# Top-k attention into a gated feed-forward: two score units in one visit of the matrix engine, and a new split of the PSUM banks

## The chip, the cores and the metric

The kernel runs on one core of one Trainium2 chip. A core has a matrix engine (TensorE, "PE" in the profile, with its weight loads as "PEld"), a vector engine (VectorE, "DVE"), a scalar engine (ScalarE, "ACT"), a general engine (GpSimd, "POOL") and DMA queues. Matrix products land in PSUM, a small memory of eight banks of 512 float32 columns on each of 128 partitions. The metric is the device time of one execution in microseconds (us), as the median of several runs; lower is better.

## The reference, cut to what matters

```python
# attention: batch 8, heads 8, sequence S = 576, head_dim D = 64, top_k = 32
scores = np.matmul(q, k.transpose(0, 1, 3, 2)) / np.sqrt(D)
kth    = np.partition(scores, -top_k, axis=-1)[..., -top_k:-top_k + 1]
scores = np.where(scores >= kth, scores, -1e9)
attn   = np.exp(scores - scores.max(-1, keepdims=True))
attn   = attn / (attn.sum(-1, keepdims=True) + 1e-9)
x      = np.matmul(attn, v)             # then (B, H, S, D) -> (4608 tokens, 512)
# feed-forward: w_in (512, 2048), w_out (2048, 512)
h   = x @ w_in
g   = h * np.cos(h)
out = g @ w_out
```

All of it is float32. The kernel works in *units*: 128 tokens times one pair of heads, 36 tiles of tokens times 4 pairs, 144 units in all. Each unit needs 128 x 576 scores for each of its two heads, the 32nd largest score of every row, a softmax over what is kept, and a product with `v`. Four units give a block of 128 tokens by 512 columns for the feed-forward, which is cut into *items*: 8 items of the first kind per block (`x @ w_in`, 8 matmuls of 128 columns each) and 8 of the second kind (`g @ w_out`, 2 matmuls of 512 columns each).

## The kernel before: the parts that the change touches

The program is a chain of *slots*, one for each unit. In slot i the vector engine searches the top 32 of unit i, the scalar engine masks and exponentiates unit i-1, the general engine normalises unit i-2 and splits it into 16-bit halves, the DMA transposes unit i-3, and in every odd slot the matrix engine multiplies two older units with `v`. The scores of unit i+1 are made and taken in the same slot. Items of the feed-forward fill the rest of the matrix engine. Each engine runs its instructions in the order in which this code lists them.

```python
def scores(u):                                   # one PSUM tile of four banks, one buffer
    sc = u["sc"] = ps.tile([P, 2, 2, 512], F32, tag="sc", bufs=1)
    for h in range(2):                           # halves of 288 keys
        for j in range(2):                       # the two heads, rows 0-63 and 64-127
            ...
            nc.tensor.matmul(sc[r0:r0 + rows, j, h, 0:HS], st["q"][d, q0:q0 + rows],
                             st["k"][d, h * HS:(h + 1) * HS], start=True, stop=True)

def take_scores(u):                              # one copy of 2 x 576 to SBUF
    nc.scalar.copy(out=s..., in_=u["sc"]...[:, :, 0:HS])

def values(us):                                  # P@V of two units into one bank of the "mm" pool
    o = us[0]["o"] = ps.tile([P, 512], F32, tag="mm", bufs=4)
    ...
def take_values(us):                             # xT <- that bank, 256 columns
    nc.scalar.copy(out=blk["xT"]..., in_=us[0].pop("o")[:, 0:n * P])

def ff1(blk, i):                                 # first kind; two items fill one bank
    if part % 2 == 0:
        blk["mm"] = ps.tile([P, 512], F32, tag="mm", bufs=4)
    ...                                          # 8 matmuls of 128 columns
    if part % 2: full.append((take_first, ...))  # the bank waits to be taken
def ff2(blk, i, f0):                             # second kind; eight items fill one bank
    if f0 == 0:
        blk["o"] = ps.tile([P, 512], F32, tag="mm", bufs=4)
    ...                                          # 2 matmuls of 512 columns
def take_banks():                                # scalar-engine copies of all full banks:
    while full: ...                              # g <- mm (first kind) or ob <- o (second)

def feed(n):                                     # up to n items, kinds in turn
    ff["tick"] += 1
    while n > 0 and ff["credit"] >= 1:
        ...
        ff["kind"] = 1 - kind
        n, ff["credit"] = n - 1, ff["credit"] - 1

def slot(i, u, w, x, y, z):                      # z: two older units, in odd slots
    if x: reciprocal(x)                          # DVE: first work of the slot, needs den(x)
    topk_first(u, w); ...; topk_round(u, 3)      # DVE: folds (read sc and s), searches
    if z: values(z)                              # PE
    else: feed(1)                                # PE
    scores(units[i + 1])                         # PE
    bounds(w); mask(w)                           # ACT: nb, nd, then two masks
    take_banks()                                 # ACT
    if z: take_values(z)                         # ACT
    take_scores(units[i + 1])                    # ACT
    exponentials(w)                              # ACT: two exps, then den
    ...
    transposes(y); gate(1); normalise(x); split(x); write_halves(x)
    feed(2); take_banks()                        # PE, then ACT
    reduce_first(); reduce_second()              # POOL: range reduction for the cosine
    feed(3)                                      # PE
    sines(2)                                     # ACT: x <- sin of a reduced tile, or of two

for i in range(NU + 1):
    ff["credit"] = min(ff["credit"] + 4.1, 5.0)
    ...
```

Of the kernel before, what the change touches and what calls it, by code (L numbers as in the profile page):

```python
# [10 lines left out]
F32 = mybir.dt.float32  # L11
# [6 lines left out]
P = 128  # L18
# [13 lines left out]
def kernel(  # L32
# [9 lines left out]
    nc = tc.nc  # L42
    ctx.enter_context(tc.manual_schedule())
    B, H, D, S = qT.shape
# [48 lines left out]
        w_out.append(w)  # L93
        chunks.append((moe_w_out[f * P : (f + 1) * P, :], w))
    CHUNKS, XB = 8, 4
    ff = {"live": 0, "tick": 0, "now": 0, "credit": 0.0, "end": False, "kind": 0}

    wq = {"next": 0, "loaded": deque(), "second": deque(), "third": deque(), "done": 0, "ready": 0}

# [92 lines left out]
    def load_v(b, hp):  # L192
# [7 lines left out]
        for j in range(2):  # L200
# [2 lines left out]
                in_=v[b, MAIN:S, hp * P + j * D : hp * P + (j + 1) * D],  # L203
            )

    def scores(u):
        sc = u["sc"] = ps.tile([P, 2, 2, 512], F32, tag="sc", name="sc", bufs=1)
        for h in range(2):
            for j in range(2):
                d = slice(j * D, (j + 1) * D)  # L210
                for b, q0, rows, r0 in u["parts"]:
                    st = pairs[b, u["hp"]]
                    nc.tensor.matmul(  # L213
                        sc[r0 : r0 + rows, j, h, 0:HS],
                        st["q"][d, q0 : q0 + rows],
                        st["k"][d, h * HS : (h + 1) * HS],
                        start=True,
                        stop=True,
                    )

    def take_scores(u):
        s = u["s"] = work.tile([P, 2, S], F32, tag="s", name="s", bufs=4)
        nc.scalar.copy(  # L223
            out=s.rearrange("p j (h w) -> p (j h) w", h=2),
            in_=u["sc"].rearrange("p j h w -> p (j h) w")[:, :, 0:HS],
        )
        if not u["folds"]:
            del u["sc"]

    def fold(u, op):  # L230


        s, sc = u["s"], u["sc"]
        if op == ALU.max:
            u["rest"] = work.tile([P, 2, S], F32, tag="rest", name="rest", bufs=1)
        else:
            del u["sc"]
        i = int(op == ALU.min)
        nc.vector.tensor_tensor(  # L239
            out=u["rest"][:, :, i * HS : (i + 1) * HS], in0=sc[:, :, 0, 0:HS], in1=s[:, :, HS:S],  # L240
            op=op,
        )

# [126 lines left out]
    def transposes_now(u):  # L370

        s = u.pop("s").rearrange("p j k -> p (j k)")
        tp = ps.tile([P, 2, 2, 512], F32, tag="sc", name="tp", bufs=1)
        tt = ps.tile([P, 512], F32, tag="mm", name="tt", bufs=4)
        for c in range(2 * NT + 1):
            j, k = divmod(c, NT + 1)
            to = tt[:, 0:P] if c == NT else tp[:, 0, j, k * P : (k + 1) * P]
            nc.tensor.transpose(to, s[:, c * P : (c + 1) * P], ident)
        pT = u["pT"] = work.tile([P, 2 * NT + 1, P], F32, tag="pT", name="pT", bufs=3)
        for j in range(2):  # L380
            at = j * (NT + 1)
            nc.scalar.copy(
                out=pT[:, at : at + NT].rearrange("p c q -> p (c q)"), in_=tp[:, 0, j]
            )
        nc.scalar.copy(out=pT[:, NT], in_=tt[:, 0:P])

    def values(us):


        o = us[0]["o"] = ps.tile([P, 512], F32, tag="mm", name="o", bufs=4)  # L390
        for i, u in enumerate(us):
            pT = u.pop("pT")
            for b, _, rows, r0 in u["parts"]:
                st = pairs[b, u["hp"]]
                r = slice(r0, r0 + rows)
                to = slice(i * P + r0, i * P + r0 + rows)
                for c in range(NT + 1):
                    for j in range(2):
                        d = slice(j * D, (j + 1) * D)
                        if c < NT:  # L400
                            lhsT, rhs = st["v"][:, c, d], pT[:, j * (NT + 1) + c, r]
                        else:
                            lhsT, rhs = st["v_tail"][:, d], pT[:, NT, r]
                        nc.tensor.matmul(o[d, to], lhsT, rhs, start=c == 0, stop=c == NT)  # L404

    def take_values(us):
        blk, hp, n = block_of[us[0]["tok"]], us[0]["hp"], len(us)
        if "xT" not in blk:
            blk["xT"] = work.tile([P, NP, P], F32, tag="xT", name="xT", bufs=5)
        nc.scalar.copy(  # L410
            out=blk["xT"][:, hp : hp + n].rearrange("p h q -> p (h q)"),
            in_=us[0].pop("o")[:, 0 : n * P],
        )
        blk["left"] -= n
        blk["tick"] = ff["tick"]
# [21 lines left out]
    sined = deque()  # L437
    full = deque()

    def ff1(blk, i):  # L440
        w = blk["w"]
        nf = 256 // w
        part = i % 4
        if part == 0:
            blk["g"].append(ffw.tile([P, 1024], F32, tag="g", name="g", bufs=CHUNKS))
            ff["live"] += 1
        if part % 2 == 0:
            blk["mm"] = ps.tile([P, 512], F32, tag="mm", name="mm", bufs=4)
        g, mm = blk["g"][-1], blk["mm"]
        for a in range(nf):  # L450
            f = i * nf + a
            at = (part % 2 * nf + a) * w
            for c in range(NC):
                nc.tensor.matmul(  # L454
                    mm[:, at : at + w],
                    w_in[f // FC][:, c, (f % FC) * P : (f % FC + 1) * P],
                    blk["xT"][:, c],
                    start=c == 0,
                    stop=c == NC - 1,
                )  # L460
        if part % 2 == 0:
            return
        full.append((take_first, blk, g, mm, part // 2))

    def take_first(blk, g, mm, half):
# [55 lines left out]
    def ff2(blk, i, f0):  # L521
        w = blk["w"]
        if f0 == 0:
            blk["o"] = ps.tile([P, 512], F32, tag="mm", name="o2", bufs=4)
        o = blk["o"]
        per = 1024 // w
        for f in range(f0, f0 + 2):
            g = blk["g"][f // per]
            at = (f % per) * w + i * P
            nc.tensor.matmul(  # L530
                o, g[:, at : at + P], w_out[f], start=f == 0, stop=f == NF - 1
            )
        if f0 + 2 < NF:
            return
        full.append((take_second, blk, i, o))

    def take_second(blk, i, o):
# [23 lines left out]
    def feed(n):  # L561

        ff["tick"] += 1
        while n > 0 and ff["credit"] >= 1:
            for kind in (ff["kind"], 1 - ff["kind"]):
                if (can_first, can_second)[kind]():
                    break
            else:
                return
            if kind == 0:  # L570
                ff1(*first.popleft())
            else:
                ff2(*second.popleft())
            ff["kind"] = 1 - kind
            n, ff["credit"] = n - 1, ff["credit"] - 1

    last = {}  # L580
    for i, u in enumerate(units):
        for part in u["parts"]:
            last[part[0], u["hp"]] = i
    at_slot = {}
    order = [(b, hp) for b in range(B) for hp in range(NP)]
    for n in range(NP, len(order)):
        i = last[order[n - 5]] - 1 if n >= 5 else 0
        at_slot.setdefault(max(i, NP + 2), []).append((load_qk, *order[n]))
        i = last[order[n - 6]] if n >= 6 else 0
        at_slot.setdefault(max(i + 5 - i % 2, NP + 2), []).append((load_v, *order[n]))  # L590

    for hp in range(NP):
# [1 line left out]
    for hp in range(2, NP):  # L594
        at_slot[hp - 2].append((load_qk, 0, hp))

    EARLY, LAST = 2 * NP, NU - NP

    for i, u in enumerate(units):
        u["n"] = i
# [41 lines left out]
    def slot(i, u, w, x, y, z):  # L644
        if x:
            reciprocal(x)
        if u:
            topk_first(u, w)
            decode_second(2)
        if u:  # L650
            topk_round(u, 1)
            topk_round(u, 2)
            topk_round(u, 3)
        if z:
            values(z)
        else:
            feed(1)
        if i + 1 < NU:
            scores(units[i + 1])

        if w:
            bounds(w)
            mask(w)
        take_banks()
        if z:
            take_values(z)
        if i + 1 < NU:
            take_scores(units[i + 1])
        if w:
            exponentials(w)  # L670
        for load, b, hp in at_slot.get(i, []):
            load(b, hp)
        load_weights(2)
        if y:
            transposes(y)
        gate(1)
        if x:
            normalise(x)
            split(x)
            write_halves(x)  # L680
        feed(2)
        take_banks()
        decode_third()
        decode_first(2)
        reduce_first()
        reduce_second()
        feed(3)
        sines(2)
# [39 lines left out]
        take_values([w])  # L728
        feed(2)

    tt = ps.tile([P, 512], F32, tag="mm", name="warm", bufs=4)
    for _ in range(12):
        nc.tensor.transpose(tt[:, 0:P], ident, ident)
    load_qk(0, 0)
# [4 lines left out]
    decode_first(3)  # L739
    for i in range(NU + 1):  # L740
        ff["end"] = i >= NU
        ff["credit"] = min(ff["credit"] + 4.1, 5.0)
        ff["now"] += 1
        wq["ready"] = wq["done"]
        u, w = (units[i - n] if 0 <= i - n < NU else None for n in range(2))
# [55 lines left out]
```

## Time and profile before

| quantity | value |
|---|---|
| time, median of 3 runs | 1526.04 us (1524.19 to 1526.63) |
| span of the profiled execution | 1522.8 us |
| PE busy | 1433.9 us (94%) |
| DVE busy | 1417.3 us (93%) |
| POOL busy | 1107.0 us (73%) |
| ACT busy | 1069.3 us (70%) |
| mean granted TensorE clock | 0.965 of full speed |

How to read it: "busy" is the time in which an engine has an instruction in execution. Matmuls are pipelined and their ends are modelled, so a busy PE isn't a PE at its peak; for PE the distances between starts say more. The profile counts two PE records for each float32 matmul of the program. A wait in a list of waits is put down to the instruction that came last. In the code above, `[P, 2, 576]` scores are `s`, the row sums `den`, the bounds for the mask `nb`, the feed-forward's copies of a bank `g` (first kind) and `ob` (second kind).

### The profile page before, as it was taken

What the parts mean: (1) busy time and instruction counts of PE and PEld (TensorE: products, weight loads), DVE (VectorE), ACT (ScalarE), POOL (GpSimd) and SP (SyncE); (2) the same over time, 40 slices, a digit from 0 to 9 for tenths busy, and PEclk for the clock granted to TensorE, in tenths of its full rate; (3) what the DMA queues carried; (4) which work ended last, traced back from release to release, by engine and by line L of the source; (5) the groups of instructions that cost most, each with busy time, mean ns of one, the idle gap of its engine ahead of it and who ended that gap; (6) DMA issues with size and microseconds to landing.
All of it is one profiled execution on the core that took longest, in us unless ns stands there. A gap on an engine that the chain in (4) does not pass through costs nothing.

```text
span 1522.8 us, 30130 instructions
## 1 busy us (share of the span) xinstructions
PE 1433.9 (94%) x10360; PEld 1023.1 (67%) x10360; DVE 1417.3 (93%) x4689; ACT 1069.3 (70%) x2120; POOL 1107.0 (73%) x838
## 2 busy tenths in 40 slices
PE   4577798999999999999999999999999999999998
PEld 3464466676767676767676767676767676767575
DVE  7999999999999999999999999999999999999721
ACT  7888667676767677767676777676777777776731
POOL 4777958777878787878787878777777777787600
PEclk6688899999999999999999999999999999999999
DMA  8432365536664655554665455645554456544200
GB/s 271 141 93 83 96 169 166 163 117 160 170 165 111 152 144 165 161 148 137 165 171 138 126 148 165 177 121 159 164 163 132 133 142 167 139 141 114 70 10 14
DMA packets 371754, 212.20 MB, mean 139 GB/s; under 512 B 321296, under 2 KB 337937, under 8 KB 371601
## 3 DMA queue, kind: packets, MB, share of 16 engines
q1 hardware_dynamic: 366192, 200.63, 48.0%
q10 hardware_dynamic: 5408, 9.65, 1.8%
q8 instruction: 81, 1.33, 0.4%
q14 instruction: 73, 0.59, 0.1%
HBM read 45.09 MB, written 87.29 MB: 87 GB/s over the span
## 4 chain that ended last, share of the span: by engine, by line
PE 70%; ACT 13%; DVE 10%; DMA 3%; issue 2%; SPq 1%; POOL 0%; ACTq 0%; POOLq 0%; DVEq 0%
PE mm L454 30%; PE o L530 23%; PE sc L213 8%; PE o L404 8%; DVE top L299 4%; DVE rest L302 3%; ACT s L329 2%; ACT x L511 2%; ACT s L321 2%; DMA pT<-rows 2%; ACT s L223 1%; ACT L511 1%; DVE rest L239 1%; DVE w_out L138 1%; ACT nd L312 1%
## 5 line engine op out<-in xcount | busy, mean ns | idle before, releaser
L299 DVE MAX8 top<-rest 128x8 f32<-128x288 f32 (+1 forms) x1656 | 682.2, 461 | 0.0
L454 PEld LDWEIGHTS mm<-xT,w_in 128*128 128x128 f32 x4608 | 545.0, 193 | 102.2 <-issue 91.8
L454 PE MATMUL mm<-xT,w_in 128*128 128x128 f32 x4608 | 565.2, 278 | 4.3 <-ACT xT L410 4.2
L530 PE MATMUL o<-w_out,g 128*128 128x512 f32 x1152 | 541.8, 603 | 4.0 <-POOL w_out L148 3.9
L302 DVE MATCH_REPLACE8 rest<-top,rest 128x288 f32<-128x288 f32 (+1 forms) x1104 | 495.5, 457 | 0.0
L530 PEld LDWEIGHTS o<-w_out,g 128*128 128x128 f32 x1152 | 203.8, 192 | 201.2 <-issue 193.0
L343 POOL TENSOR_SCALAR s<-s,rden 128x576 f32<-128x576 f32 x288 | 212.9, 751 | 139.3 <-DVE rden L338 139.3
L355 POOL COPY halves<-s 128x2304 uint16<-128x2304 uint16 x132 | 277.8, 2105 | 35.6 <-DMA rows<-halves 28.5
L329 ACT ACTIVATE s<-s,nd 128x576 f32<-128x576 f32 x288 | 220.7, 769 | 0.4
L223 ACT COPY s<-sc 128x1152 f32<-128x1152 f32 x144 | 160.7, 1116 | 84.9 <-PE sc L213 84.7
L321 ACT ACTIVATE s<-s,nb 128x576 f32<-128x576 f32 x288 | 205.4, 760 | 0.0
L213 PE MATMUL sc<-k,q 64*128 64x288 f32 (+1 forms) x1280 | 187.3, 443 | 19.0 <-ACT s L223 8.7
L239 DVE TENSOR_TENSOR rest<-sc,s 128x576 f32<-128x576 f32 x264 | 198.7, 753 | 4.9 <-DVE rden L338 0.4
L518 POOL TENSOR_TENSOR g<-g,x 128x1024 f32<-128x1024 f32 x68 | 161.4, 2375 | 51.6 <-ACT x L511 46.9
L309 ACT ACTIVATE nb<-top 128x4 f32<-128x4 f32 x144 | 29.1, 202 | 233.5 <-DVE top L292 233.2
L404 PE MATMUL o<-pT,v 128*64 128x128 f32 (+1 forms) x2560 | 166.0, 272 | 19.2 <-DMA pT<-rows 10.7
L404 PEld LDWEIGHTS o<-pT,v 128*64 128x64 f32 x2560 | 136.4, 141 | 65.1 <-issue 36.8
L501 POOL TENSOR_TENSOR x<-g,x 128x1024 f32<-128x1024 f32 x68 | 161.0, 2367 | 5.7
L213 PEld LDWEIGHTS sc<-k,q 64*128 64x128 f32 (+1 forms) x1280 | 102.2, 183 | 81.5 <-issue 22.5
L492 POOL TENSOR_SCALAR x<-g 128x1024 f32<-128x1024 f32 x68 | 71.3, 1049 | 89.7 <-ACT g L466 89.7
L466 ACT ACTIVATE g<-mm 128x512 f32<-128x512 f32 x144 | 82.1, 582 | 48.6 <-PE mm L454 48.6
L302 DVE MATCH_VALUE_LOAD rest<-top,rest 128x8 f32 x1104 | 86.4, 78 | 0.0
(52 smaller groups left out, 1014.8 us busy)
## 6 DMA issues: line engine op xcount, KB each, us to landing
rows<-halves SPq DMA_DIRECT2D x132, 576.0 KB, 3.2
out_dram<-ob ACTq DMA_DIRECT2D x36, 256.0 KB, 2.8
q<-in_q_dram SPq DMA_DIRECT2D x31, 288.0 KB, 3.0
st<-in_moe_w_in_dram SPq DMA_DIRECT2D x16, 512.0 KB, 5.2
v<-in_v_dram SPq DMA_DIRECT2D x32, 256.0 KB, 3.1
st<-in_moe_w_out_dram SPq DMA_DIRECT2D x16, 512.0 KB, 3.5
k<-in_k_dram SPq DMA_DIRECT2D x31, 144.0 KB, 3.4
k<-in_k_dram SPq DMA_DIRECT2D x32, 128.0 KB, 3.8
```

The lines of the kernel that those rows point to most:

```text
L213: nc.tensor.matmul(sc[r0 : r0 + rows, j, h, 0:HS], st["q"][d, q0 : q0 + rows], st["k"][d, h * HS : (h + 1) * HS], start=True, stop=True,)
L223: nc.scalar.copy(out=s.rearrange("p j (h w) -> p (j h) w", h=2), in_=u["sc"].rearrange("p j h w -> p (j h) w")[:, :, 0:HS],)
L239: nc.vector.tensor_tensor(out=u["rest"][:, :, i * HS : (i + 1) * HS], in0=sc[:, :, 0, 0:HS], in1=s[:, :, HS:S], op=op,)
L299: nc.vector.max(to[:, j], src[:, j])
L302: nc.vector.match_replace(rest[:, j], to[:, j], src[:, j], NEG)
L321: nc.scalar.activation(out=s[:, j], in_=s[:, j], func=AF.Prelu, bias=nb[:, j, 1:2], scale=SCALE, alpha=FAR)
L329: nc.scalar.activation(out=s[:, j], in_=s[:, j], func=AF.Exp, bias=nd[:, j : j + 1], scale=1.0, accum_out=den[:, j : j + 1],)
L343: nc.gpsimd.tensor_scalar(out=s[:, j], in0=s[:, j], scalar1=rden[:, j : j + 1], scalar2=1.0, op0=ALU.mult, op1=ALU.mult,)
L355: nc.gpsimd.tensor_copy(out=halves, in_=s.rearrange("p (k h) -> p h k", h=2))
L404: nc.tensor.matmul(o[d, to], lhsT, rhs, start=c == 0, stop=c == NT)
L454: nc.tensor.matmul(mm[:, at : at + w], w_in[f // FC][:, c, (f % FC) * P : (f % FC + 1) * P], blk["xT"][:, c], start=c == 0, stop=c == NC - 1,)
L530: nc.tensor.matmul(o, g[:, at : at + P], w_out[f], start=f == 0, stop=f == NF - 1)
```

## The change

Scores get two tiles of two banks, so that two units can be in PSUM at once: 448 of the 576 columns lie in such a tile, and the last 128 lie in a pair of banks called `rim`, which both units share and in which P@V and the late transposes also have their place. Scores are then made for two units in one visit of the matrix engine, right behind P@V of two units, in odd slots; in even slots none are made (units of a tile that straddles two sequences are still made one at a time). The purpose is that the matrix engine changes less often between the shapes of attention and those of the feed-forward. The feed-forward is left with two banks, and its items go in twos of a kind, so that a bank of the first kind is filled in one go.

```diff
+    SB = 448
+    rim = ps.tile([P, 2, 512], F32, tag="rim", name="rim", bufs=1)
+    sc_ends = [rim[:, :, i * (S - SB) : (i + 1) * (S - SB)] for i in range(2)]
+    room = [rim[:, j, 2 * (S - SB) :] for j in range(2)]
     def scores(u):
-        sc = u["sc"] = ps.tile([P, 2, 2, 512], F32, tag="sc", name="sc", bufs=1)
-        for h in range(2):
+        sc = u["sc"] = ps.tile([P, 2, 512], F32, tag="sc", name="sc", bufs=2)
+        for to, k0, k1 in ((sc, 0, SB), (sc_ends[u["n"] % 2], SB, S)):
             for j in range(2):
 ...
     def take_scores(u):
-        nc.scalar.copy(out=s.rearrange(...), in_=u["sc"].rearrange(...)[:, :, 0:HS])
+        nc.scalar.copy(out=s[:, :, 0:SB], in_=u["sc"][:, :, 0:SB])
+        nc.scalar.copy(out=s[:, :, SB:S], in_=sc_ends[u["n"] % 2])
 ...
     def values(us):
-        o = us[0]["o"] = ps.tile([P, 512], F32, tag="mm", name="o", bufs=4)
+        o = room[0]
 ...
+    def open_bank():
+        if ff["open"] + len(full) == 2:
+            take_banks()
+        ff["open"] += 1
     def ff1(blk, i):
         if part % 2 == 0:
-            blk["mm"] = ps.tile([P, 512], F32, tag="mm", name="mm", bufs=4)
+            open_bank()
+            blk["mm"] = ps.tile([P, 512], F32, tag="mm", name="mm", bufs=2)
 ...  (ff2 in the same way)
     def feed(n):
-            ff["kind"] = 1 - kind
+            if kind != ff["kind"] or ff["half"]:
+                ff["kind"], ff["half"] = 1 - kind, 0
+            else:
+                ff["half"] = 1
 ...
+        two = i % 2 and EARLY + 2 < i < LAST + 2 and len(u["parts"]) == 1
+        scored.setdefault(i - 2 if two else i - 1, []).append(u)
 ...
     def slot(i, u, w, x, y, z):
         if z:
             values(z)
-        else:
+        made = scored.get(i, [])
+        if not made or not z:
             feed(1)
-        if i + 1 < NU:
-            scores(units[i + 1])
+        for m in made:
+            scores(m)
 ...
-        ff["credit"] = min(ff["credit"] + 4.1, 5.0)
+        ff["credit"] = min(ff["credit"] + 5.0 - 0.9 * len(scored.get(i, [])), 5.3)
```

## The prediction

> **What bounds the kernel now.** I read the busy times over stretches first, then the waits of each engine, then the timeline of one period.
>
> ```profile
> 300.00:500.00 200.00, 199.00 (x1420) 143.44 (x1418) 196.81 (x687) 141.87 (x285) 157.51 (x116) 1.00 0.53 145
> 700.00:900.00 200.00, 198.64 (x1429) 142.33 (x1426) 196.19 (x687) 147.76 (x289) 161.39 (x117) 1.00 0.55 149
> 1440.00:1480.00 40.00, 39.93 (x269) 28.39 (x268) 8.12 (x14) 17.72 (x37) 2.94 (x4) 1.00 0.04 14
> ```
>
> The columns are the stretch, its length, then PE, PEld, DVE, ACT and POOL busy. Between 300 and 1300 us PE shows no gap and DVE is busy for 98.2%: two engines are full at once. After 1440 us the attention is over and PE alone works off the feed-forward's rest.
>
> ```profile
> DVE rden L338 <- ACT den L334: 14.3, 16, 1.3
> DVE rden L338 <- POOL x L493: 0.5, 1, 0.5
> ```
>
> These are all waits of DVE in 1000 us (total, times, longest): only the first instruction of a slot waits, for `den`, and that in 16 slots of about 104. The starts of that reciprocal say the same: 9.50 us apart in nearly every slot, 10.4 to 10.9 once in eight. So a slot costs at least 9.50 us (9.41 after a stall), and 1526 us can shrink only by those stalls: slots 28 to 140 last from 321.1 to 1401.2 us, 1080.1 us for 112 slots, against 112 x 9.50 = 1064. That is 16 us, 1%, however much PE is relieved. The stall, in the timeline:
>
> ```profile
> 811.79 1.28 ACT L511 ACT_TABLE_LOAD   x1
> 813.09 2.19 ACT L511 ACTIVATE x<-x,halfpi 128x1024 f32<-128x1024 f32 x2
> 815.18 0.19 ACT L309 ACTIVATE nb<-top 128x4 f32<-128x4 f32 x1
> 815.79 1.42 ACT L321 ACTIVATE s<-s,nb 128x576 f32<-128x576 f32 x2
> 817.12 0.57 ACT L539 ACTIVATE ob<-o 128x512 f32<-128x512 f32 x1
> 817.73 0.34 ACTq L541 DMA_DIRECT2D out_dram<-ob  x1
> 818.11 0.37 ACT L410 COPY xT<-o 128x256 f32<-128x256 f32 x1 [0.41 <-ACT ob L539]
> 818.38 1.12 ACT L223 COPY s<-sc 128x1152 f32<-128x1152 f32 x1
> 819.52 1.28 ACT L329 ACT_TABLE_LOAD   x1
> 820.81 0.78 ACT L329 ACTIVATE s<-s,nd 128x576 f32<-128x576 f32 x1
> 822.47 0.29 ACT L334 ACTIVATE den<-den,eps 128x2 f32<-128x2 f32 x1
> 822.87 0.17 DVE L338 RECIPROCAL rden<-den 128x2 f32<-128x2 f32 x1 [1.07 <-ACT den L334]
> ```
>
> ACT is 71% busy, but its order is the chain of the slot: `nb`, masks, banks, `xT`, `s`, exps, `den`. After a pair of sines the exps need another table, and with `ob` in the same slot `den` is 1.07 us late.
>
> **What the skill says.** "PSUM — Partial Sum Buffer", section "Engine vs sequencer instructions": the queues of ScalarE, VectorE and GpSimd are strict FIFO. The trace agrees: at 818.11 `xT` starts behind `ob` and the issue of its DMA, though its matmuls were long done (the last began at 816.11). "ScalarE: Activation LUTs", section "What ACT_TABLE_LOAD costs": a load takes about 1283 ns; here 1.28 us. "TensorEngine Tiling (Array Packing)", section "Key Properties": a change of tiling mode drains the engine; that is what the change saves, with the price taken from the trace below. "PSUM — Partial Sum Buffer", section "PSUM bank collisions raise a hardware error": accesses are to be guarded by bank and not by address. The program of before reads and writes different banks, so its trace shows nothing of that; the changed program's waits do.
>
> **The change part by part.**
>
> *PE, removed.* Between items a visit for one unit's scores costs:
>
> ```profile
> 802.22 5.32 PE L530 MATMUL o<-w_out,g 128*128 128x512 f32 x12
> 807.46 1.24 PE L213 MATMUL sc<-k,q 64*128 64x288 f32 x8
> 808.63 1.12 PE L530 MATMUL o<-w_out,g 128*128 128x512 f32 x2
> ```
>
> Starts of single records: 429 ns between two of 512 columns in a run, 522 ns from the last one to the first score; 340 ns for the first pair of scores against 242 for the next; 332 for the last; 533 for the first of the second kind after. The excess is 93 + 98 + 90 + 104 = 385 ns a visit. Counting visits in the program's order: 142 become 84. So 58 x 0.385 = 22 us of PE go, 0.39 us in two slots. The columns are the same: pairs of 448 at 448/288 x 242 = 376 ns and of 128 at 109 (as P@V's pairs), two records each, 970 ns a unit; 4 x 242 = 968 before. Two slots of PE now: P@V 2.33, first unit 1.07 (with its 98), second 0.97, way in and out 0.28, eight items 4 x 1.79 + 4 x 1.72 = 14.03: together 18.68 us, under DVE's 19.0.
>
> *ACT, added.* Two copies for one: 896 columns and 256 at 0.83 ns each plus a start, overlapped as before: 1.06 us for 1.00. The sines come one at a time, at the end of every even slot, not in pairs every fourth: table loads in the program's order go from 74 to 132, 58 x 1.28 = 74 us. ACT has the room, but now every odd slot has a load between `s` and the exps.
>
> *Wait A: `xT` behind both units' scores.* In the changed program the copy to `xT` reads `rim`, and its wait is for the last matmul into `rim`, which is the second unit's end piece. `s` comes behind `xT` in ACT's order. With V the start of P@V: last record at V + 2.33 + 1.07 + 0.86 = V + 4.26, its latency 0.27 and the signal 0.06: `xT` at V + 4.59. Then 0.27 to `s`, 0.79 to the second copy, 0.37 to its end, 1.29 table load, 1.96 exps and `den`, 0.10 to the reciprocal (distances in the trace above): the next slot starts at V + 9.37 or later. Before, `xT` could start at V + 2.46. If P@V starts within 0.1 us of the slot, nothing is lost; every later us is a us of stall.
>
> *Wait B: the first kind has one bank.* Of the two banks, one holds `o2` through eight items. In each fourth slot (the one with `ob`) the order is P@V, scores, then only in the last feed F1 F1 F2, after the last taking of banks. So this F1 bank is copied in the next slot, behind `nb` and the masks; with T that slot's reciprocal, `nb` is at T + 1.85 (832.27 to 834.15 less 0.03), the copy 1.96 later, its end 0.58 later, T + 4.39. The next F1 pair must wait for it: T + 4.45. Behind it PE does F1 F1 (0.10 + 3.57), F2 F2 (3.43), the way into P@V (0.09): V = T + 11.64. The next slot starts at T + 9.5, so P@V is 2.14 us late there, and by wait A the slot after it starts at T + 11.64 + 9.37 = T + 21.01: a stall of 2.0 us.
>
> *Four slots together.* Then 9.45 for the even slot (P@V comes 18.68 after the last, near the start of its slot again), then the `ob` slot: `xT` at 1.85 + 1.96 + 0.57 + 0.42 = 4.80, `s` 5.07, then 0.79 + 0.37 + 1.29 + 1.96 + 0.10: 9.58. Sum 21.01 + 9.45 + 9.58 = 40.04 us for four slots, against 1080.1/28 = 38.58 before: +1.46.
>
> *Sum.* 28 such periods in slots 28 to 140; in three the tile straddles two sequences, scores are made singly, wait A is 0.97 us shorter, so 39.1. 25 x 40.04 + 3 x 39.1 = 1118, less 1080: +38 us. Slots 20 to 27 have the same waits in part: +2. The work left for the end is the same: 33 and 32 items stand behind the last attention matmul. 1526 + 40 = 1566 us.
>
> **Rivals.**
> *PE relieved, DVE reaches its floor.* If wait B were covered, P@V would run ahead, `den` would be in time, and every slot would be 9.5: 1526 - 16 = 1510. For it: PE has 0.3 us to spare in two slots, and the credits and twos look chosen for eight items in two slots. Against it: wait B stands in the order of ACT, and no spare 0.3 us makes up for 2.1.
> *The stalls cancel.* The old stall (1.0 us in eight slots) goes, the new one is smaller because P@V is not as late as I make it or because `xT` needs only P@V: then `s` could start at V + 3.4, 1.4 us earlier, the stall in four slots is 0.6, and the time 1526 within 5 us.
> *More waits.* The sine at the end of an even slot ends at about T + 1.87 of the next, where `nb` wants to start at 1.85; POOL's gate follows it; the transposed halves land some 1.5 us before P@V wants them. If one of these slips, another 0.5 us in four slots: 1580.
>
> **Range and chances.** The working gives 1566. Errors are one-sided in size: full relief is 1510, slips give 1580. I set 1544 to 1580. The line for slower by 2% is 1556.6, that is +31 against my +40; a quarter of my weight is on smaller stalls. Faster by 2% (1495) lies below DVE's floor.
>
> **What would show it.** Reciprocals about 9.5, 11.5, 9.4, 9.6 us apart in turn; `rden` waiting for `den` some 2 us in 28 slots; PE idle before `mm`, with ACT `g` named, 1.7 to 2.4 us in each fourth slot; `xT` starting only behind the second unit's scores; ACT_TABLE_LOAD doubled; score visits at 84. I'm wrong if `xT` starts before the second unit's scores are through, if PE doesn't wait for `g` behind the masks, or if the slots stay at 9.5.

## The result and the profile after

| | before | after |
|---|---|---|
| time, median (of runs of the same comparison) | 1525.12 us | 1596.68 us |
| ratio, 95% interval | | 1.0473 (1.0450 to 1.0496) |
| slots 28 to 140, by the starts of the reciprocal | 1080.1 us | 1148.4 us |
| start of slot 28 / from slot 140 to the end | 321.1 / 121.6 us | 327.5 / 120.2 us |
| ACT_TABLE_LOAD | 74 x 1.28 us | 132 x 1.28 us |

The change makes the kernel 4.7% slower. The prediction had said slower, 1566 us, with 1580 as the upper end; the measured time lies above its range.

The busy times over stretches of the kernel after (stretch, length, then PE, PEld, DVE, ACT, POOL busy, granted TensorE clock, DMA share, GB/s), to be held against the same stretches of before:

```profile
300.00:500.00 200.00, 189.80 (x1309) 136.45 (x1306) 185.20 (x647) 144.25 (x295) 144.58 (x107) 0.97 0.51 143
700.00:900.00 200.00, 189.42 (x1354) 137.62 (x1354) 186.10 (x652) 150.95 (x301) 146.96 (x108) 0.98 0.52 140
```

Neither of the two engines that were full is full any more: PE is at 95%, DVE at 93%, and the clock is no longer 1.00. The waits of the kernel after, over its whole span (engine, line waited for, total us, times, longest), name a ring:

```profile
DVE rden L343 <- ACT den L339: 110.0, 43, 9.1
ACT xT L414 <- PE rim L220: 105.5, 58, 4.5
PE mm L465 <- ACT g L478: 56.6, 32, 1.9
```

DVE waits for ACT (`den`), ACT for PE (`xT` behind the scores' end pieces in `rim`), PE for ACT (the copy `g` that frees the bank of the first kind). Between 300 and 1300 us, the stretch of the list of before in the prediction, the first of these is 73.7 us in 29 waits, against 14.3 in 16. Each engine has long idle times, and each is ended by another engine: such a ring is read by asking which wait is the first in a period. The reciprocals show where the slots get long:

```profile
788.75 0.15 DVE L343 RECIPROCAL rden<-den 128x2 f32<-128x2 f32 x1
800.34 0.17 DVE L343 RECIPROCAL rden<-den 128x2 f32<-128x2 f32 x1 [2.00 <-ACT den L339]
809.75 0.15 DVE L343 RECIPROCAL rden<-den 128x2 f32<-128x2 f32 x1
819.38 0.17 DVE L343 RECIPROCAL rden<-den 128x2 f32<-128x2 f32 x1
828.79 0.15 DVE L343 RECIPROCAL rden<-den 128x2 f32<-128x2 f32 x1
842.00 0.17 DVE L343 RECIPROCAL rden<-den 128x2 f32<-128x2 f32 x1 [3.63 <-ACT den L339]
```

These lines of the timeline (start, length, engine, what) give the slots 11.59, 9.41, 9.63, 9.41, 13.21 us. The pattern is the predicted one (11.5, 9.4, 9.6, then 9.5), but of the late slots 15 take 13.2 to 13.4 us. The PE timeline of such a case, and ahead of it the same wait four slots earlier:

```profile
783.72 3.84 PE L465 MATMUL mm<-xT,w_in 128*128 128x128 f32 x32 [1.93 <-ACT g L478]
787.39 3.60 PE L543 MATMUL o<-w_out,g 128*128 128x512 f32 x8
```

```profile
818.22 3.60 PE L543 MATMUL o<-w_out,g 128*128 128x512 f32 x8
823.75 5.47 PE L465 MATMUL mm<-xT,w_in 128*128 128x128 f32 x32 [1.93 <-ACT g L478]
829.05 3.60 PE L543 MATMUL o<-w_out,g 128*128 128x512 f32 x8
832.58 1.09 PE L408 MATMUL rim<-pT,v 128*64 128x128 f32 x16
836.74 0.39 PE L220 MATMUL rim<-k,q 64*128 64x128 f32 x4
```

and ACT in the stretch of the second one:

```profile
823.12 0.57 ACT L478 ACTIVATE g<-mm 128x512 f32<-128x512 f32 x1
837.18 0.37 ACT L414 COPY xT<-rim 128x256 f32<-128x256 f32 x1 [2.93 <-PE rim L220]
838.65 1.28 ACT L334 ACT_TABLE_LOAD   x1
841.60 0.29 ACT L339 ACTIVATE den<-den,eps 128x2 f32<-128x2 f32 x1
```

`g` ends at 823.69 and PE starts at 823.75 after 1.93 us of idle. The 32 records that follow then take 829.05 - 823.75 = 5.30 us. P@V begins at 832.58, the second unit's end piece comes at 836.74, `xT` at 837.18, and `den` ends 4.7 us after that. In the period before, after the same wait of 1.93 us (783.72), the 32 records took 787.39 - 783.72 = 3.67 us. What differs is in the view of stretches, with the granted clock behind the five busy times:

```profile
783.70:787.10 3.40, 3.38 (x30) 3.39 (x31) 3.40 (x13) 2.84 (x7) 0.75 (x1) 1.00 1.11 299
824.40:827.70 3.30, 3.30 (x18) 3.30 (x17) 3.30 (x13) 2.17 (x7) 0.30 (x1) 0.50 1.15 245
```

The clock was halved for 3.41 us after the second wait, and not after the first. Between slots 28 and 140 there are 16 such windows, in 28 periods; 15 of them lie before a slot of 13.2 to 13.4, the first before one of 11.8 us.

### The profile page after: what moved, and what is told of

Read it like the earlier page. It is cut to its first block, busy times and chain, and to the rows that moved or that the text cites. A ratio compares the mean times of both kernels' runs of the same rounds, so it can differ in the third digit from the quotient of the medians.

```text
span 1596.1 us, 30173 instructions
## 1 busy us (share of the span) xinstructions
PE 1446.7 (91%) x10360; PEld 1041.4 (65%) x10360; DVE 1418.5 (89%) x4689; ACT 1154.5 (72%) x2322; POOL 1104.6 (69%) x838
## 4 chain that ended last, share of the span: by engine, by line
PE 39%; ACT 23%; DVE 20%; POOL 11%; issue 4%; DMA 2%; SPq 1%; DVEq 0%; ACTq 0%; POOLq 0%
PE mm L465 15%; PE o L543 12%; PE rim L408 6%; DVE top L304 6%; DVE rest L244 6%; ACT s L334 5%; DVE rest L307 5%; ACT s L326 5%; PE sc L220 4%; POOL g L530 3%; POOL halves L360 3%; ACT s L230 2%; ACT L334 2%; POOL s L348 2%; ACT nd L317 2%
## 5 line engine op out<-in xcount | busy, mean ns | idle before, releaser
L465 PE MATMUL mm<-xT,w_in 128*128 128x128 f32 x4608 | 586.7, 287 | 64.6 <-ACT g L478 56.6
L465 PEld LDWEIGHTS mm<-xT,w_in 128*128 128x128 f32 x4608 | 561.1, 201 | 122.2 <-ACT g L478 80.5
L543 PE MATMUL o<-w_out,g 128*128 128x512 f32 x1152 | 522.4, 596 | 6.1 <-POOL w_out L148 4.0
L543 PEld LDWEIGHTS o<-w_out,g 128*128 128x128 f32 x1152 | 208.8, 191 | 218.1 <-issue 208.0
L408 PEld LDWEIGHTS rim<-pT,v 128*64 128x64 f32 x2560 | 136.4, 142 | 78.8 <-ACT nb L314 22.7
L408 PE MATMUL rim<-pT,v 128*64 128x128 f32 (+1 forms) x2560 | 164.7, 274 | 23.5 <-ACT pT L389 13.4
L220 PE MATMUL sc<-k,q 64*128 64x448 f32 (+1 forms) x640 | 149.8, 591 | 14.5 <-DMA k<-in_k_dram 8.7
L230 ACT COPY s<-sc 128x896 f32<-128x896 f32 x144 | 129.3, 898 | 6.8 <-PE sc L220 6.8
L343 DVE RECIPROCAL rden<-den 128x2 f32<-128x2 f32 x144 | 22.5, 156 | 111.2 <-ACT den L339 110.0
L414 ACT COPY xT<-rim 128x256 f32<-128x256 f32 (+1 forms) x78 | 27.6, 354 | 119.6 <-PE rim L220 105.5
```

Source lines behind the costliest of these rows:

```text
L220: nc.tensor.matmul(to[r0 : r0 + rows, j, 0 : k1 - k0], st["q"][d, q0 : q0 + rows], st["k"][d, k0:k1], start=True, stop=True,)
L465: nc.tensor.matmul(mm[:, at : at + w], w_in[f // FC][:, c, (f % FC) * P : (f % FC + 1) * P], blk["xT"][:, c], start=c == 0, stop=c == NC - 1,)
L543: nc.tensor.matmul(o, g[:, at : at + P], w_out[f], start=f == 0, stop=f == NF - 1)
```

## The experiments

The theory after the result: two waits make a late slot of 11.6 us (A: `xT` behind both units' scores; B: the first kind's bank copied behind the next slot's masks), and B's idle time costs PE half its clock in 16 of 28 cases. The rivals: the doubled table loads or wait A set the slot whatever the bank does; the extra 1.6 us of the longest slots come from elsewhere. All ratios are to the kernel before.

| run | what it changes in the kernel after | us | ratio (95% interval) | slots 28 to 140, us |
|---|---|---|---|---|
| e1_take_at_end | all banks taken also at a slot's end | 1525.68 | 1.0002 (0.9995 to 1.0009) | 1077.1 |
| e2_keep_busy | PE kept busy through wait B | 1576.33 | 1.0337 (1.0322 to 1.0353) | 1124.6 |
| e3_xT_behind_one | `xT` behind one unit's scores | 1544.77 | 1.0132 (1.0117 to 1.0147) | 1096.1 |
| e4_single_visits | scores of one unit a visit | 1551.99 | 1.0177 (1.0162 to 1.0193) | 1099.7 |
| e5_kinds_in_turn | items one of a kind | 1641.95 | 1.0763 (1.0744 to 1.0781) | 1189.2 |
| e6_first_at_end | first kind taken at a slot's end, and e3 | 1514.68 | 0.9930 (0.9916 to 0.9944) | 1067.7 |
| e7_xT_first | e6, and `xT` ahead of the banks | 1513.75 | 0.9931 (0.9914 to 0.9947) | 1067.2 |
| e8_pairs | e7, and sines in pairs | 1523.16 | 0.9991 (0.9982 to 1.0000) | 1071.6 |
| e9_single_and_end | e10, and scores of one unit a visit | 1526.72 | 1.0006 (0.9997 to 1.0014) | 1076.2 |
| e10_end_alone | first kind taken at a slot's end | 1517.64 | 0.9942 (0.9928 to 0.9956) | 1070.5 |

### The half clock: e2_keep_busy

```diff
         if not made or not z:
             feed(1)
+        if not made and any(f[0] is take_first for f in full):
+            for _ in range(9):
+                nc.tensor.matmul(room[1][:, 0:P], ident, ident, start=True, stop=True)
```

The nine matmuls add work whose results nobody reads; nothing of the kernel is left out.

> The changed kernel with nine matmuls of the identity (results unused, about 2.0 us) on PE in the place where it waits for the bank; the wait itself stays. My theory (14 of the late slots last 13.2 and not 11.6 us because the clock is halved for 3.4 us after PE stood idle): no half-clock windows, all late slots near 11.6, 1597 - 14 x 1.63 = 1574 us (1568 to 1582). Rival (the extra 1.6 us come from something else, a DMA landing or POOL): the 13.2 us slots stay, 1597 us or more, for PE has more to do.

PE of this run around the wait:

```profile
808.13 3.60 PE L543 MATMUL o<-w_out,g 128*128 128x512 f32 x8
811.57 2.17 PE L683 MATMUL rim<-ident 128*128 128x128 f32 x18
813.67 3.84 PE L465 MATMUL mm<-xT,w_in 128*128 128x128 f32 x32
817.35 3.60 PE L543 MATMUL o<-w_out,g 128*128 128x512 f32 x8
```

The added records fill the gap, the 32 records take 817.35 - 813.67 = 3.68 us, no half-clock window is left between 250 us and slot 140, and the late slots are 11.58 or 11.59 but for a few near the singly scored units. The kernel became 20.4 us shorter although PE does more. So the difference between 11.6 and 13.2 is the clock, and nothing that lands or waits elsewhere.

### Wait A: e3_xT_behind_one

```diff
-        for m in made:
+        for m in made[:1]:
             scores(m)
         ...
             take_values(z)
+        for m in made[1:]:
+            scores(m)
         take_scores(units[i + 1])
```

> The changed kernel with the copy to xT recorded between the two units' scores: the order on every engine stays, but xT waits for the first unit's end piece alone and the second unit's end piece waits for xT. My theory (wait A is on the path of every late slot): the late slots lose 0.97 us, 11.6 to 10.6 and 13.2 to 12.2, so 28 x 0.97 = 27 us, 1569 us (1562 to 1578). Rival (the lateness of P@V alone counts, or the second end piece now waits as long as was won): 1590 to 1600 us.

It won 51.9 us, twice what I expected. PE and ACT of this run:

```profile
801.27 3.84 PE L465 MATMUL mm<-xT,w_in 128*128 128x128 f32 x32 [1.05 <-ACT g L478]
808.48 1.09 PE L408 MATMUL rim<-pT,v 128*64 128x128 f32 x16
```

```profile
812.10 0.37 ACT L414 COPY xT<-rim 128x256 f32<-128x256 f32 x1 [1.86 <-PE rim L220]
```

`xT` starts 3.62 us after P@V and not 4.60, and the late slots are 10.61, 0.97 less than 11.58, as expected. What I had missed: the period gets shorter by 0.97 us while PE's work in it stays, so PE also idles less in the next wait. The idle time fell from 1.93 to 1.05 us, and with it went all half-clock windows between 250 us and slot 140. So the cure of wait A won its own 27 us and also the 24 us or so by which e2, which cures the clock alone, shortens slots 28 to 140: the two costs aren't independent.

### Wait B: e1_take_at_end, e10_end_alone, e6_first_at_end

```diff
         feed(3)
+        take_banks()                # e1
+        take_banks(take_first)      # e10 and e6: only while a first-kind bank stands in front
         sines(2)
```

> The changed kernel with one more taking of the full banks, at the end of every slot. My theory (the first kind's bank, copied only behind the next slot's masks, holds PE up for 2.1 us in every fourth slot, which makes P@V late, and the idle PE loses half its clock): both go. Reciprocals 9.4 to 9.6 us apart in all slots, no half-clock window between 250 and 1400 us, 1515 us (1508 to 1525), so faster than the kernel before. Rival (the doubled table loads and the copy to xT behind both units' scores set the slot, the bank doesn't): little changes, above 1565 us.

The late slots of 11.6 and 13.2 are gone, but for three of 11.3 to 11.6 near the singly scored units, and the half clock with them. But one slot in four is 9.85, and the time is that of before and not the 1515 us that I expected. ACT of this run shows why:

```profile
737.37 0.60 ACT L553 ACTIVATE ob<-o 128x512 f32<-128x512 f32 x1 [1.96 <-PE o L543]
738.36 1.28 ACT L523 ACT_TABLE_LOAD   x1 [0.40 <-ACT ob L553]
739.66 1.15 ACT L523 ACTIVATE x<-x,halfpi 128x1024 f32<-128x1024 f32 x1
740.71 0.19 ACT L314 ACTIVATE nb<-top 128x4 f32<-128x4 f32 x1
```

My edit took second-kind banks at the slot's end too. `ob` then waited 1.96 us on PE, and table load, sine and `nb` behind it came late: an instruction put early into ACT's order isn't early if its input is late. With first-kind banks alone:

> The changed kernel with the banks of the first kind taken also at the end of every slot, and nothing else. My theory (the bank is the cause of the late P@V, and xT behind both units costs only when P@V is late): all slots 9.4 to 9.7 us, no half-clock windows, 1516 us (1511 to 1521). Rival (xT behind both units costs by itself, and the earlier run that had both cures owed its time to that one): 1522 us or more.

Its waits of DVE for `den` between 330 and 1390 us:

```profile
DVE rden L343 <- ACT den L339: 5.0, 5, 1.8
```

1517.64, inside the expected range: this one added call takes 79 us off the kernel after. The slots are 9.4 to 9.7 as expected, except for five, of which three near the singly scored units take 10.6 to 11.3. Wait A and the doubled table loads stay in it, so neither sets the slot whatever the bank does. A then costs little, because P@V is in time: in the next run, which cures A too, slots 28 to 140 are 2.8 us shorter. Together with e3's edit:

> The changed kernel with the banks of the first kind (not of the second) taken also at the end of every slot, and xT recorded between the two units' scores. In the first of my runs the end-of-slot copy of a second-kind bank waited about 2 us on PE and pushed the sines into the next slot's bounds, and that left slots of 9.85 us. My theory: with that gone and xT behind one unit, every slot is 9.4 to 9.6 us, 1513 us (1508 to 1520). Rival (PE has no room: 18.7 us in two slots plus the wait of the new block for xT): slots of 9.7 on average, 1525 us as the kernel before.

One stretch of this run:

```profile
700.00:900.00 200.00, 197.76 (x1434) 141.14 (x1430) 199.06 (x695) 161.76 (x323) 158.34 (x117) 1.00 0.58 153
```

Between 330 and 1390 us DVE waits for `den` for only 1.9 us, in 2 slots, and it is busy for 99.5% of the stretch (98.1% before). Slots 28 to 140 take 1067.7 us, against 1064 for 112 x 9.50: the floor that the prediction had named. It is faster than both kernels, by 0.7% against the one before.

### What is left: e7_xT_first and e8_pairs

```diff
-        take_banks()
         if z:
             take_values(z)
+        take_banks()
```

> As the run before it, with xT copied ahead of the banks in ACT's order, so that the new block's first matmuls wait about 0.9 us less in every fourth slot. My theory: DVE is the bound already, so at most the few slots over 9.5 shrink: 1512 us, within 3 us of the run before it. Rival (PE is the bound there): 1505 us or less relative to it, 0.7 us in every fourth slot, some 20 us.

Within a us of e6, as expected where DVE is the bound. The second run lets a sine wait up to four slots for another (`waiting[0][3] + 4` for `+ 2`).

> As the run before it, with sines in pairs again (they wait up to four slots for a second one): table loads fall from 132 to about 80. My theory: ACT has the room wherever den is in time, so this gives nothing beyond the ob slots of 9.6: 1510 us (1506 to 1516). Rival (the doubled table loads are a cost by themselves): 10 us or more below the run before it.

Table loads fell to 72, and the time rose by 9.4 us: both expectations missed. ACT's busy time fell from 1152.8 to 1070.5 us and bought nothing. In the profile slots 28 to 140 are 4.4 us longer, among them slots of 9.98 in which the two sines stand ahead of `nb`; the rest lies at the start and the end (3.5 and 1.6 us), and its cause stays open. The doubled loads look like the change's largest added cost (74 us), but in e7 slots 28 to 140 stand 3 us above DVE's floor of 1064, so there they leave almost nothing to win. That doesn't clear them in the kernel after: in its late slot the load of 838.65 stands between `s` and the exps, on the path from `xT` to `den`, and no run took it out there.

### The parts undone: e4_single_visits, e5_kinds_in_turn, e9_single_and_end

```diff
-        two = i % 2 and EARLY + 2 < i < LAST + 2 and len(u["parts"]) == 1
+        two = False and i % 2 and EARLY + 2 < i < LAST + 2 and len(u["parts"]) == 1   # e4, e9
```

> The changed kernel with the scores of every unit made in a visit of its own again; the new banks and the items in twos stay. My theory: the wait for the bank stays, but a score visit of 1.4 us stands ahead of it, so PE idles 0.7 us and not 2.1 and keeps its clock, and xT waits for one unit: late slots 10.6 us, 1545 us (1535 to 1560), though PE has 22 us more to do. Rival (the two banks and the twos cost it all whatever the scores do): 1585 to 1600 us.

Late slots of 10.61, 0.77 us of idle PE in the wait for the bank, no half clock, 1552 us: with the double visit undone and the bank wait kept, the kernel is faster than with both. The items' order:

```diff
-            if kind != ff["kind"] or ff["half"]:
-                ff["kind"], ff["half"] = 1 - kind, 0
-            else:
-                ff["half"] = 1
+            ff["kind"] = 1 - kind                          # e5
```

> The changed kernel with the items' kinds in turn again, one of each; the two banks and the double score visits stay. By the order of the program the first kind then finds its bank behind the masks in three of four even slots and not in two of four. My theory (the wait is for the bank): more late slots, 1610 us (1590 to 1640). Rival (the twos themselves make P@V late, the banks suffice): faster than the changed kernel, 1560 us or less.

1642, just above the range (1590 to 1640), but not for the reason that I gave. PE's waits between 330 and 1390 us:

```profile
PE o L543 <- POOL g L530: 62.5, 12, 5.4
PE mm L465 <- ACT g L478: 19.0, 23, 1.9
```

The wait for the bank's copy is 19.0 us in all, against 46.8 in the kernel after. The largest is a new one, up to 5.4 us long: items of the second kind wait for the `g` that POOL makes for them. So this run shows that the twos are better here, and not that the banks are the cause. Last, e10 with single visits:

> As that run, with the scores of every unit in a visit of its own: the double visit undone, its 22 us of PE back. My theory (with the bank wait gone the double visit is worth what the change meant, up to DVE's floor; without it PE is over DVE's 19.0 us in two slots): 1525 us (1518 to 1532), 5 to 15 us above the run before it. Rival (the double visit is worth nothing since DVE sets the slot): within 2 us of the run before it.

1526.72 against 1517.64: 9.1 us, of which 5.7 lie in slots 28 to 140 by the profiles. With the bank wait gone, the double visit is worth something; with it, it was a loss.

## Why the prediction was wrong in size

- **Bound and floor**: right. DVE's 9.50 us a slot is what e6 and e7 reach, and PE's relief could bring 1% at most.
- **PE, removed**: right in kind. e9 against e10 puts 9.1 us on it, less than the 22 us of PE time: with single visits PE is full (busy for 199.65 of the 200 us from 700 to 900, 196.66 in e10), but slots 28 to 140 take 1076.2 us, so only 12 us lie above DVE's floor.
- **Wait A**: right, to 0.01 us (4.60 from the start of P@V to `xT`, 4.59 in the working); e3 shows that it is on the path of the late slots.
- **Wait B**: right in mechanism and in the moment at which PE starts again (4.36 or 4.37 us after the reciprocal in all 28 periods, as 823.75 less 819.38; the working 4.45). **Its next term failed**: "Behind it PE does F1 F1 (0.10 + 3.57)". That is full clock. The 32 records took 3.67 us in 12 of the 28 periods and 5.30 in the other 16, because there the idle time that the wait makes had halved the clock. P@V then starts 13.20 us after the reciprocal and not 11.57 (the working 11.64), and the late slot takes 13.2 and not 11.6. I carried a duration over from a stretch in which PE showed no gap to one in which I had just predicted that it idles for 2 us.
- **Sum**: late slots of 11.6 (11.5 predicted) and 13.2; `ob` slots 9.63 (9.58); the others 9.41. Predicted for slots 28 to 140: 1118, measured 1148.4. Of the 30 us, e2 puts 24 on the clock (1148.4 - 1124.6 in the profiles). Some 4 us are three slots after the singly scored ones, 10.6 to 11.4 and not 9.6, which I had treated as `ob` slots in time; the other 2 to 3 us stay open. The start cost 6.4 us and not 2; what it is made of stays open too.
- **Rivals**: full relief failed by wait B, as argued against it. "The stalls cancel" failed: `xT` did wait for both units. "More waits" pointed the right way with the wrong cause, and its 1580 closed the range too low.
- **Chances**: slower by over 2% was the likeliest, and it is what came.

## What to carry to other kernels

When a change frees an engine that is level with another, look first at what its work waits for and where that stands in the other engine's order: here the copy that gives a bank back stood behind two masks, and one added call that takes it earlier turned 4.7% slower into 0.6% faster. The cures of two waits in one ring can't be summed: alone, e10 won 79 us and e3 52, together 82. And where a change lets the matrix engine idle for about 2 us, as here, work out the matmuls behind the gap at half clock too.

## What the runs showed of the hardware

In the Trainium skill, "TensorE: Matmul & The Clock Gate", section "Why this matters for your kernels", warns of idle gaps over some 3 us, and its Part 1 tells of windows of 3413 ns that run free. The windows agree: between slots 28 and 140 the half-clock stretches last 3.41 us and start whole multiples of it apart. The length doesn't: a gap of some 2 us was enough. I laid the grid of windows over the starts of the PE records of the kernel after between slots 28 and 140 (a record of 512 columns counts as 0.43 us from its start, so the wait of 1.93 us in the profile, where ends are modelled, becomes 2.09; gaps under 0.3 us are left out). In 16 windows 2.09 us were idle, and each was followed by half clock; in 20 it was 0.53 to 2.03 us, and none was. So of two equal gaps the one that fell into a single window cost 1.6 us of clock and the one that straddled two cost none, which fits late slots of now 11.6 and now 13.2. The measurement decides here. Idle time alone doesn't fix the limit everywhere: at 196.3 us, before slot 28 and ahead of other work, a window with 1.89 us of idle was followed by half clock. Where the limit lies, and what else it hangs on, was not tried.
